# Fewer loads at the head of a retention and soft-mixture kernel: eight of them issued later, by ScalarE

## The chip, the cores and the metric

The kernel runs on one core of one Trainium2 chip. Its time is the device time of one execution in microseconds (us); the median of the runs is what counts. A core has five engines that run their own instruction streams and meet through semaphores: TensorE (PE, matrix products; PEld is its loading of stationary operands), VectorE (DVE), ScalarE (ACT), GpSimd (POOL) and SyncE (SP, which here only issues DMAs). Data come from HBM into SBUF through 16 DMA engines; products arrive in PSUM, which has eight banks.

## The reference

Two stages follow each other for batch 8, 8 heads, 576 positions and head width 64. The first is retention, causal attention without a softmax, with a decay by distance for each head:

```python
scores = scale * np.matmul(q, k.transpose(0, 1, 3, 2))
gamma = 1.0 - 2.0 ** (-5.0 - np.arange(H, dtype=np.float32))
Dmat = np.where(rel >= 0, gamma[:, None, None] ** rel[None, :, :], 0.0)
x = np.matmul(scores * Dmat[None], v)      # then (B, S, 512)
```

The second takes x (8 x 576 x 512) through four attention experts of width 64, of which each position uses the best two by a gate:

```python
logits = x @ w_gate                        # best 2 of 4, weights by softmax
for e in range(E):
    q = x @ wq[e]; k = x @ wk[e]; v = x @ wv[e]
    a = softmax(causal(scale * (q @ k.transpose(0, 2, 1))))
    out += gate_weight[e] * (a @ v @ wo[e])
```

All is float32. The inputs are q, k, v of the first stage (laid out as tiles `xf` and `vkf` before the launch) and the weights (`wraw`).

## The kernel before

The positions are cut into 36 tiles of 128 (`NT`), three of which form a group (`NG` = 12 groups). The program is one loop over j (groups, with three more rounds to drain) and i (0 to 2), so that tile n = 3j + i passes through the first stage while the projections of group j − 1, the scores of group j − 2 and the output of group j − 3 are worked on.

For tile n in the first stage these functions are called, in this order around the loop: `qk(n+1)` (products of q and k of the tile on TensorE, copied out of PSUM by ScalarE into `p`, line 144, and masked by GpSimd, line 147), `old(n)` (the part from the running state, copied out by ScalarE, line 169), `own(n)` (the part from the tile itself, added by VectorE, lines 187 and 188), `state(n+1)` (the running state; TensorE, then adds on VectorE, line 128), `scale(n)` (decay factors from the table `gi`, line 200; VectorE for the first three tiles, GpSimd after), `split(n)` (rounding into a high part `xh` by ScalarE, line 210, and its remainder `xl` by GpSimd, line 211), `table(n+1)` (the next piece of the table, four small activations, line 99) for the first tiles, and `decay` (line 107), which multiplies the v of a later tile by powers of the decay, on VectorE for tiles 0 to 2, on GpSimd behind. For n = 2 `qk(3)` stands behind `own(2)` instead of ahead of `old(2)`.

`weights(w)` (line 227) rounds one of the four weight matrices into a high and a low part in the same way: ScalarE makes the high part (`wh`, line 235), VectorE or, for `q`, GpSimd the low one (`wl`, line 236). `k` is done after tile 1, `q` and `v` after tile 2, `o` after tile 5. With `v` goes the gate's small matrix `rg`. `proj` (`pj`, line 250) needs `k` and `q` and all three tiles of its group and first runs in the round n = 3; `vproj` (`pv`, line 274) needs `v` and first runs at n = 4.

Loads: `load(n, 0)` brings the q and k of a tile (`x`, 512 KB, three buffers), `load(n, 1)` its v and k in another layout (`vk`, 512 KB, four buffers), `fetch(w)` a weight matrix (`raw`, 512 KB). All are issued on SyncE. A load into a buffer that is in use waits for its last reader: `x3` takes the buffer of `x0`, which `old(0)` reads last, `x4` that of `x1`, and `vk4` that of `vk0`.

What sets the order: the instructions of TensorE, VectorE, ScalarE and GpSimd run in the order in which the program writes them (`ORDERED`). SyncE's order is chosen by the planner of the framework, which may put a load that is ready ahead of one that still waits. PSUM is handed out as eight banks in turn (`bank`), so that a new product waits for whoever empties the bank that was taken eight calls before.

Of the kernel before, what the change touches and what calls it, by code (L numbers as in the profile page):

```python
# [27 lines left out]
def f(ap):  # L28
    return ap.bitcast(F32)
# [9 lines left out]
def units(g):  # L39
    out = []  # L40
    for n in range(3 * g, 3 * g + 3):
        out += [(n, 0), (n, 1)] if n % 9 == 8 else [(n, None)]
    return out
# [3 lines left out]
def kernel(ctx: ExitStack, tc: tile.TileContext, xf, vkf, wraw, gi_d, con_d, out):  # L47
    nc = tc.nc
# [8 lines left out]
    v = nc.vector  # L57
# [25 lines left out]
    HALF = [slice(0, 64), slice(64, 128)]  # L83
    X, VK, P, S_, XR = {}, {}, {}, {}, {}

    def load(n, w):
        if n >= NT:
            return
        if w == 0:
            X[n] = x = ld.tile([128, 2, 4, 128], F32, name="x", tag="x")  # L90
            nc.sync.dma_start(x, xf[n])
        else:
            VK[n] = vk = ld.tile([128, 2, 2, 4, D], F32, name="vk", tag="vk", bufs=4)
            nc.sync.dma_start(vk, vkf[n])

    def table(c):
        t0, C = 128 * c, 128 if c < 4 else 64
# [3 lines left out]
    def decay(n, e=None):  # L101
        if n >= NT:
            return
        vv = VK[n][:, :, 0]
        k = chunks(n)[0][1]
        gm = gam[:, 8:9] if k == 8 else gam[:, k:k + 2]
        (e or gp).tensor_mul(vv, vv, gm.unsqueeze(3).to_broadcast([128, 2, 4, D]))  # L107
# [22 lines left out]
    def qk(n):  # L130
        if n >= NT:
            return
        x = X[n]
        ps = [bank([128, 2, 2, 64], "qk") for g in range(2)]
        for s in range(2):
            i = slice(64 * s, 64 * s + 64)
            for u in range(2):
                for g in range(2):
                    for r in range(2):
                        h = 2 * r + u  # L140
                        mm(ps[g][HALF[r], s, u], x[HALF[g], 1, h, i], x[HALF[g], 0, h, i], start=True, stop=True)  # L141
        P[n] = p = sa.tile([128, 2, 2, 2, 64], F32, name="p", tag="p")
        for g in range(2):
            act(p[:, g], ps[g], AF.Copy)  # L144
        for r in range(2):
            w = p[HALF[r]].rearrange("p g s u i -> p (g s u) i")
            gp.affine_select(w, w, pattern=[[0, 8], [1, 64]], base=0, channel_multiplier=-1,  # L147
                             compare_op=OP.is_ge, fill=0.0)
# [3 lines left out]
    def old(n):  # L152
        if n >= NT:
            return
        ps = [bank([128, 2, 128], "old") for g in range(2)]
        x = X[n]
        R[n] = x32 = sa.tile([128, 2, 2, 128], F32, name="x32", tag="x32", bufs=2)
        ch = chunks(n)
        f0 = 64 if ch[0][1] == 0 else 0
        for s, (b, k) in enumerate(ch):  # L160
            i = slice(64 * s, 64 * s + 64)
            if k:
                for r in range(2):
                    for g in range(2):
                        for u in range(2):
                            mm(ps[g][HALF[u], r, i], S_[b, k - 1][HALF[g], r, u], x[HALF[g], 0, 2 * r + u, i],  # L166
                               start=True, stop=True)
        for g in range(2):
            act(x32[:, g, :, f0:], ps[g][:, :, f0:], AF.Copy)

    def own(n):
        if n >= NT:
            return
        ps = [bank([128, 2, 128], "own") for r in range(2)]
        p, vk, x32 = P.pop(n), VK[n], R[n]
        ch = chunks(n)
        f0 = 64 if ch[0][1] == 0 else 0
        for s in range(2):
            i = slice(64 * s, 64 * s + 64)
            for g in range(2):  # L180
                for r in range(2):
                    for u in range(2):
                        mm(ps[r][HALF[u], g, i], vk[HALF[r], s, 0, 2 * g + u], p[HALF[r], g, s, u],  # L183
                           start=True, stop=True)
        for r in range(2):
            if f0:
                v.tensor_copy(x32[:, :, r, :f0], ps[r][:, :, :f0])
            v.tensor_add(x32[:, :, r, f0:], x32[:, :, r, f0:], ps[r][:, :, f0:])  # L188

    def scale(n, e=None):  # L190
        if n >= NT:
            return
        e = e or gp
        x32 = R[n].rearrange("p g r i -> p (g r) i")
        k = chunks(n)[0][1]
        if k == 8:
            w = x32.rearrange("p c (s i) -> p c s i", s=2)
            e.tensor_mul(w, w, gi[:, :, 512:].unsqueeze(2).to_broadcast([128, 4, 2, 64]))
        else:
            e.tensor_mul(x32, x32, gi[:, :, 64 * k:64 * k + 128])  # L200

    def split(n, e=None):
        if n >= NT:
            return
        g, l0 = n // 3, 128 * (n % 3)
        if n % 3 == 0:
            XR[g] = (sa.tile([128, 4, GW], F32R, name="xh", tag="xh"), sa.tile([128, 4, GW], F32R, name="xl", tag="xl"))
        xh, xl = XR[g]
        x32 = R.pop(n).rearrange("p g r i -> p (g r) i")
        act(xh[:, :, l0:l0 + 128], x32, AF.Copy)  # L210
        (e or gp).tensor_sub(xl[:, :, l0:l0 + 128], x32, f(xh[:, :, l0:l0 + 128]))  # L211
# [6 lines left out]
    TSZ = {1: 11 * 128, 2: 15 * 128, 3: 9 * 128, 4: 9 * 128}  # L218
    rg = const.tile([128, 4, E], F32, name="rg")

    def fetch(w):
        o, kc, n = WCUT[w]
        z = {"k": 1, "q": 2, "v": 3, "o": 4}[w]
        RAW[w] = raw = sb.tile([128, PSZ[z]], F32, name="raw", tag=f"p32{z}")[:, :kc * n].rearrange("p (k w) -> p k w", k=kc)
        nc.sync.dma_start(raw, wraw[:, o:o + kc * n].rearrange("p (k w) -> p k w", k=kc))

    def weights(w, e=None):
        o, kc, n = WCUT[w]
        raw = RAW[w]
        wt = n if w != "v" else NWV  # L230
        hi = const.tile([128, kc, wt], F32R, name="wh" + w)
        lo = const.tile([128, kc, wt], F32R, name="wl" + w)
        W[w] = (hi, lo)
        for r, cs in [(raw, slice(0, n))] + ([(rg, slice(n, wt))] if w == "v" else []):
            act(hi[:, :, cs], r, AF.Copy)
            (e or v).tensor_sub(lo[:, :, cs], r, f(hi[:, :, cs]))
# [248 lines left out]
    def stage(j, i):  # L485
        g, o = j - 1, j - 3
        if 0 <= g < NG:
            if i == (0 if j == 1 else 2):
                for p in range(2):
                    for w in "kq":  # L490
                        yield from proj(g, w, p)
            else:
                for ti in (2,) if i == 1 else (0, 1):
                    yield from vproj(3 * g + ti)
        if 0 <= o < NG and i < 2:
            for d in (2 * i, 2 * i + 1):
                yield from outproj(o, d)
# [8 lines left out]
    load(2, 0)  # L506
    load(2, 1)
    fetch("k")
    fetch("q")
    nc.sync.dma_start(rg, wraw[:, 4096:].rearrange("p (k w) -> p k w", k=4))  # L510
    load(3, 1)
    fetch("v")
    nc.sync.dma_start(mask[:, 512:], con_d[:, 220:])
    decay(0, v)
    qk(0)
# [1 line left out]
    for j in range(NG + 3):  # L517
        us = units(j - 2) if 0 <= j - 2 < NG else []
        for i in range(3):
            n = 3 * j + i  # L520
            if n < 2:
                decay(n + 1, v)
            if n != 2:
                qk(n + 1)
            old(n)
            work = stage(j, i)
            here = us[i:i + 1] if i < 2 else us[2:]
            soft = [scores(u) for u in here[:1]]
            for sc in soft:
                next(sc)  # L530
            own(n)
            if n == 2:
                qk(3)
            state(n + 1)
            for u in here[1:]:
                soft.append(scores(u))
                next(soft[-1])
            load(n + 3, 0)
            load(n + 4, 1)
            if n == 0:  # L540
                fetch("o")
            scale(n, v if n < 3 else None)
            if 2 < n + 2 and i < 2:
                decay(n + 2)
            for u, sc in zip(here, soft):
                for _ in sc:
                    next(work, None)
                normal(u)
            split(n)
            if 0 < n + 1 < 5:  # L550
                table(n + 1)
            if i == 2:
                decay(n + 2)
            if n == 1:
                weights("k")
            if n == 2:
                weights("q", gp)
                weights("v")
            if n == 5:
                weights("o")  # L560
            run(work)
        for u in us:
            run(turn(u))
        if 0 <= j - 1 < NG:
            gate(j - 1)
        for u in us:
            values(u, u[0] == NT - 1)
# [56 lines left out]
```

## Time and profile before

| | |
|---|---|
| median of three runs | 470.75 us (470.01 to 472.14) |
| the profiled execution | 470.5 us |
| its span, first to last instruction | 468.5 us |
| mean granted TensorE clock | 0.967 |
| HBM read, written | 40.26 MB, 9.44 MB |

The profile is that of one execution. Its page gives each engine's busy time and groups of instructions by line; the timeline lists instructions in order of time, neighbours of one line merged, each with its start, its length, the engine, what it writes and reads, and in square brackets the idle time ahead of it with what ended it. "issue" there means that the engine waited for nothing that the profile shows. Issuing a DMA is not counted as busy time of an engine. Of the DMAs the page says how long they took from issue to landing. The clock column gives the share of full TensorE speed that was granted. The profiled execution took 2.0 us more than its span, for what lies around the first and last instruction.

### The profile page before, as it was taken

Reading aid. Unit: us, or ns where it says so; the run is one execution under the profiler, and the core shown is the slowest. Engines: PE = TensorE matmul, PEld = TensorE weight load, DVE = VectorE, ACT = ScalarE, POOL = GpSimd, SP = SyncE. Lnnn points to the kernel's source line nnn. Section 1 sums busy time; section 2 is a strip of 40 time slices with the busy share of each in tenths; the row PEclk is TensorE's granted clock in tenths of the full one; section 3 lists DMA queues with packets and bytes.
Section 4 is the critical chain, followed back from the end, with each engine's and each line's share of the span. In section 5 each row is a group of like instructions: output and inputs, shape, how many; then the busy total and the mean of one; then the engine's idle time right before and its main releaser. Section 6 shows DMA issues by size and latency. Waiting matters only on the chain.

```text
span 468.5 us, 18762 instructions
## 1 busy us (share of the span) xinstructions
PE 436.8 (93%) x7876; PEld 397.9 (85%) x7876; DVE 273.0 (58%) x1069; ACT 286.4 (61%) x834; POOL 216.1 (46%) x272
## 2 busy tenths in 40 slices
PE   7589879999999999999999999999999999999786
PEld 4478769889879989889979999889979999897476
DVE  1562773864685654864775654854775654746650
ACT  2545466584685476584686576685686576664752
POOL 5477665563653555563653455553553453202001
PEclk8769899999999999999999999999999999999869
DMA  8953441242252153252352153242241010010101
GB/s 286 406 200 105 171 135 48 93 160 91 92 186 65 50 186 110 92 165 86 94 167 83 41 193 111 92 163 88 93 162 44 5 52 18 2 69 2 69 0 69
DMA packets 18899, 50.89 MB, mean 109 GB/s; under 512 B 2304, under 2 KB 9088, under 8 KB 18816
## 3 DMA queue, kind: packets, MB, share of 16 engines
q1 hardware_dynamic: 18816, 49.71, 31.3%
q8 instruction: 62, 1.02, 0.9%
q14 instruction: 21, 0.17, 0.1%
HBM read 40.26 MB, written 9.44 MB: 106 GB/s over the span
## 4 chain that ended last, share of the span: by engine, by line
PE 79%; ACT 7%; DVE 4%; DMA 4%; issue 3%; POOL 1%; SPq 1%; ACTq 0%; POOLq 0%; DVEq 0%
PE pj L250 22%; PE pv L274 11%; PE pt L419 8%; PE po L473 8%; PE ss L348 7%; PE ys L445 6%; PE own L183 4%; DMA x<-xf 4%; PE qk L141 4%; PE st L119 3%; PE old L166 2%; ACT p L379 2%; PE ys L452 2%; DVE sm L391 2%; PE ys L449 2%
## 5 line engine op out<-in xcount | busy, mean ns | idle before, releaser
L211 POOL TENSOR_TENSOR xl<-x,xh 128x512 fp32r<-128x512 f32 x36 | 46.1, 1280 | 89.3 <-ACT xh L210 89.3
L379 ACT ACTIVATE p<-p,nm 128x128 f32<-128x128 f32 (+8 forms) x144 | 79.7, 559 | 10.4 <-DVE nm L368 9.5
L368 DVE CUSTOM_DVE_ANT_0 p<-ss,mask 128x128 f32<-128x128 f32 (+7 forms) x128 | 51.0, 454 | 29.0 <-PE ss L348 28.5
L463 POOL CAST yh<-y 128x256 fp32r<-128x256 f32 (+1 forms) x38 | 14.4, 380 | 106.4 <-ACT y L462 106.4
L399 ACT ACTIVATE p<-p,sm 128x64 f32<-128x64 f32 (+4 forms) x72 | 37.0, 556 | 42.0 <-DVE sm L393 42.0
L423 DVE COPY pth<-pt 128x512 f32<-128x512 f32 (+2 forms) x52 | 31.4, 618 | 48.2 <-PE pt L419 47.8
L147 POOL TENSOR_SCALAR_AFFINE_SELECT p<-p 64x512 f32<-64x512 f32 x72 | 48.7, 676 | 20.3 <-ACT p L144 17.7
L419 PE MATMUL pt<-con,p 128*128 128x128 f32 x360 | 45.1, 287 | 5.4 <-DVE nm L373 3.3
L419 PEld LDWEIGHTS pt<-con,p 128*128 128x128 f32 x360 | 43.3, 149 | 6.1 <-DVE nm L373 3.4
L200 POOL TENSOR_TENSOR x<-x,gi 128x512 f32<-128x512 f32 x29 | 37.4, 1290 | 20.4 <-DVE x L188 19.5
L348 PE MATMUL ss<-k,q 64*64 64x64 f32 (+7 forms) x512 | 41.7, 409 | 2.2 <-ACT ot L476 2.2
L183 PEld LDWEIGHTS own<-p,vk 64*64 64x64 f32 x1152 | 28.5, 142 | 13.4 <-issue 10.4
L445 PE MATMUL ys<-pth,vn 128*64 128x128 f32 (+1 forms) x640 | 39.8, 257 | 0.0
L183 PE MATMUL own<-p,vk 64*64 64x64 f32 x1152 | 30.4, 229 | 6.6 <-ACT xh L210 2.8
L107 POOL TENSOR_TENSOR vk<-vk,con 128x512 f32<-128x512 f32 x33 | 35.4, 1074 | 0.3 <-DMA vk<-vkf 0.3
L391 DVE TENSOR_SCALAR sm<-sm 128x4 f32<-128x4 f32 (+1 forms) x40 | 15.5, 388 | 30.6 <-ACT p L379 30.0
L425 ACT ACTIVATE pth<-pt 128x512 f32<-128x512 f32 (+2 forms) x52 | 27.2, 541 | 9.3 <-PE pt L419 9.3
L210 ACT ACTIVATE xh<-x 128x512 fp32r<-128x512 f32 x36 | 22.2, 617 | 17.2 <-POOL x L200 9.6
L445 PEld LDWEIGHTS ys<-pth,vn 128*64 128x64 f32 x640 | 29.6, 139 | 1.5 <-issue 1.5
L401 DVE TENSOR_SCALAR p<-p,sm 128x64 f32<-128x64 f32 (+4 forms) x104 | 29.1, 333 | 1.4
L141 PEld LDWEIGHTS qk<-x 64*64 64x64 f32 x1152 | 21.6, 141 | 9.6 <-issue 7.0
L119 PE MATMUL st<-vk 64*64 64x64 f32 x1024 | 25.8, 232 | 4.3 <-DVE vk L107 2.2
(94 smaller groups left out, 1069.8 us busy)
## 6 DMA issues: line engine op xcount, KB each, us to landing
x<-xf SPq DMA_DIRECT2D x36, 512.0 KB, 4.0
vk<-vkf SPq DMA_DIRECT2D x36, 512.0 KB, 5.3
out<-ot SPq DMA_DIRECT2D x48, 192.0 KB, 2.0
raw<-wraw SPq DMA_DIRECT2D x4, 512.0 KB, 9.4
gi<-gi SPq DMA_DIRECT2D x1, 256.0 KB, 8.1
con<-con SPq DMA_DIRECT2D x1, 110.0 KB, 3.9
mask<-con SPq DMA_DIRECT2D x1, 32.0 KB, 8.5
rg<-wraw SPq DMA_DIRECT2D x1, 8.0 KB, 9.3
```

The source lines that it names most:

```text
L119: mm(ps[r][HALF[g], s, u], vk[HALF[r], s, 1, h], vk[HALF[r], s, 0, h], start=True, stop=True)
L141: mm(ps[g][HALF[r], s, u], x[HALF[g], 1, h, i], x[HALF[g], 0, h, i], start=True, stop=True)
L147: gp.affine_select(w, w, pattern=[[0, 8], [1, 64]], base=0, channel_multiplier=-1, compare_op=OP.is_ge, fill=0.0)
L183: mm(ps[r][HALF[u], g, i], vk[HALF[r], s, 0, 2 * g + u], p[HALF[r], g, s, u], start=True, stop=True)
L211: (e or gp).tensor_sub(xl[:, :, l0:l0 + 128], x32, f(xh[:, :, l0:l0 + 128]))
L250: mm(ps, ww[:, kc, p * 128:(p + 1) * 128], xx[:, kc, c], start=(i == 0), stop=(i == 11))
L274: mm(ps, xx[:, kc, l0:l0 + 128], ww[:, kc], start=(i == 0), stop=(i == 11))
L348: mm(ps[e][HALF[p]], q[p][HALF[z], l0 + 64 * s:l0 + 64 * s + 64], k[p][HALF[z], kb:kb + ws[e]], start=True, stop=True)
L368: v.tensor_tensor_reduce(p32[:, e, :ws[e]], ps[e], mask[:, 576 - ws[e]:], -1.0, BIG, OP.add, OP.min, nm[:, e:e + 1])
L379: act(p32[:, e, :ws[e]], p32[:, e, :ws[e]], AF.Exp, bias=bias[e], scale=-1.0, accum_out=sm[:, 0, e:e + 1])
L419: nc.tensor.transpose(pt[:, i], src, ident)
L445: mm(py[HALF[z], p], VN[n0 + j][:, e * D:(e + 1) * D], src, start=(j == 0), stop=False)
```

## The change

Ahead of the loop, the loads of `rg` and `v` are gone and `load(3, 0)` is called there. In the loop, `load(n+3, 0)` and `load(n+4, 1)` are called on SyncE only from n = 3 on. The loads of `x4`, `vk4`, `rg` and `v` are issued by ScalarE behind `split(1)`, and those of `x5`, `vk5`, `vk6` and `o` behind `split(2)`, in each case ahead of `table`. `weights("v")` moves from n = 2 to n = 3, behind `table(4)`.

```diff
-    def load(n, w):
+    def load(n, w, e=None):
+        e = e or nc.sync
...
-            nc.sync.dma_start(x, xf[n])
+            e.dma_start(x, xf[n])
...
-            nc.sync.dma_start(vk, vkf[n])
+            e.dma_start(vk, vkf[n])
...
-    def fetch(w):
+    def fetch(w, e=None):
...
-        nc.sync.dma_start(raw, wraw[:, o:o + kc * n].rearrange("p (k w) -> p k w", k=kc))
+        (e or nc.sync).dma_start(raw, wraw[:, o:o + kc * n].rearrange("p (k w) -> p k w", k=kc))
...
     fetch("k")
     fetch("q")
-    nc.sync.dma_start(rg, wraw[:, 4096:].rearrange("p (k w) -> p k w", k=4))
+    load(3, 0)
     load(3, 1)
-    fetch("v")
     nc.sync.dma_start(mask[:, 512:], con_d[:, 220:])
...
-            load(n + 3, 0)
-            load(n + 4, 1)
-            if n == 0:
-                fetch("o")
+            if n > 2:
+                load(n + 3, 0)
+                load(n + 4, 1)
             scale(n, v if n < 3 else None)
...
             split(n)
+            if n == 1:
+                load(4, 0, nc.scalar)
+                load(4, 1, nc.scalar)
+                nc.scalar.dma_start(rg, wraw[:, 4096:].rearrange("p (k w) -> p k w", k=4))
+                fetch("v", nc.scalar)
+            if n == 2:
+                load(5, 0, nc.scalar)
+                load(5, 1, nc.scalar)
+                load(6, 1, nc.scalar)
+                fetch("o", nc.scalar)
             if 0 < n + 1 < 5:
                 table(n + 1)
...
             if n == 2:
                 weights("q", gp)
+            if n == 3:
                 weights("v")
```

## The prediction, made before the changed kernel was run

> **What bounds the kernel now.** I read the page first, then busy time by stage.
>
> ```profile
> span 468.5 us, 18762 instructions
> ```
>
> ```profile
> 0.00:32.00 32.00, 21.24 (x574) 17.04 (x575) 12.77 (x33) 14.62 (x38) 17.38 (x35) 0.74 0.83 305
> 200.00:400.00 200.00, 196.69 (x3667) 182.43 (x3668) 121.54 (x492) 131.38 (x386) 97.76 (x116) 1.00 0.29 97
> ```
>
> The two rows are stretches of the run; behind the length stand busy time of PE, PEld, DVE, ACT, POOL, then granted clock, DMA share and GB/s. From 200 to 400 us TensorE is busy for 196.69 of 200 us, so nothing but TensorE counts there. In the first 32 us it is busy for 21.24, at a mean clock of 0.74, and the DMA engines are at 0.83. This head is all that the change touches; I take it that what follows the first projection shifts with the projection's start. So the question is: when does the first projection (`pj`) start, and at which clock? The timeline of the head, engine by engine, answers the first half: TensorE, ScalarE, VectorE, GpSimd (start, length, then what ran, and in brackets the wait before it).
>
> ```profile
> 21.61 1.05 PE L183 MATMUL own<-p,vk 64*64 64x64 f32 x32 [2.77 <-ACT xh L210]
> ...
> 25.79 1.12 PE L141 MATMUL qk<-x 64*64 64x64 f32 x28 [0.57 <-DMA x<-xf]
> 28.42 0.37 PE L141 MATMUL qk<-x 64*64 64x64 f32 x2 [1.51 <-issue]
> ...
> 30.32 1.14 PE L119 MATMUL st<-vk 64*64 64x64 f32 x30
> 31.39 1.35 PE L250 MATMUL pj<-xh,whk 128*128 128x384 f32 x4
> ```
>
> ```profile
> 20.01 0.63 ACT L210 ACTIVATE xh<-x 128x512 fp32r<-128x512 f32 x1 [2.91 <-DVE x L200]
> 20.55 1.26 ACT L99 ACTIVATE gi<-gi,con 128x128 f32<-128x128 f32 x4
> 21.71 1.04 ACT L235 ACTIVATE whk<-raw 128x1024 fp32r<-128x1024 f32 x1
> 22.66 0.63 ACT L169 ACTIVATE x<-old 128x256 f32<-128x256 f32 x2
> 24.38 0.66 ACT L144 ACTIVATE p<-qk 128x256 f32<-128x256 f32 x2 [1.09 <-PE qk L141]
> 27.11 0.63 ACT L210 ACTIVATE xh<-x 128x512 fp32r<-128x512 f32 x1 [2.07 <-DVE x L200]
> 27.65 1.26 ACT L99 ACTIVATE gi<-gi,con 128x128 f32<-128x128 f32 x4
> 28.82 1.04 ACT L235 ACTIVATE whq<-raw 128x1024 fp32r<-128x1024 f32 x1
> 29.76 1.04 ACT L235 ACTIVATE whv<-raw 128x1024 fp32r<-128x1024 f32 x1
> 30.71 0.20 ACT L235 ACTIVATE whv<-rg 128x16 fp32r<-128x16 f32 x1
> 30.81 0.63 ACT L144 ACTIVATE p<-qk 128x256 f32<-128x256 f32 x2
> ```
>
> ```profile
> 22.79 1.22 DVE L236 TENSOR_TENSOR wlk<-raw,whk 128x1024 fp32r<-128x1024 f32 x1 [2.87 <-ACT whk L235]
> 23.93 0.74 DVE L188 TENSOR_TENSOR x<-x,own 128x256 f32<-128x256 f32 x2
> 25.23 0.88 DVE L128 TENSOR_TENSOR s<-st,s 128x128 f32<-128x128 f32 x4 [0.56 <-PE st L119]
> 26.04 0.98 DVE L200 TENSOR_TENSOR x<-x,gi 128x512 f32<-128x512 f32 x1
> ```
>
> ```profile
> 27.89 1.27 POOL L211 TENSOR_TENSOR xl<-x,xh 128x512 fp32r<-128x512 f32 x1 [1.41 <-ACT xh L210]
> 29.11 1.04 POOL L107 TENSOR_TENSOR vk<-vk,con 128x512 f32<-128x512 f32 x1
> ```
>
> Three routes arrive at the first projection (31.39) almost together. **TensorE's own:** its waits of 2.77, 0.57 and 1.51 us in front of `own(2)`, `qk(4)` and the last of `qk(4)`; then it works on without a pause past 31.39. **GpSimd's:** the rounding of tile 2 (`xh`, 27.11), its remainder `xl` (27.89), the decay of `vk4` (29.11, done at 30.15), and at once `state(4)` on TensorE. **ScalarE's:** from 20.01 to 23.29 without a gap (`xh`, table, `whk`, eviction of `old(2)`); `whk` lets VectorE make `wlk` (22.79), behind which stand the adds of `own(2)` and `state(3)` and the scaling (26.04); that gives `xh` of tile 2 at 27.11, and again ScalarE without a gap up to `p(4)` at 30.81. Counted from the code, the eight PSUM banks go round, and the first projection takes the one that `p(4)` empties. So a shorter wait on TensorE alone brings the projection forward by nothing: GpSimd's and ScalarE's routes must get shorter too. The change works on the first and puts eight DMA issues into the other two.
>
> **The change, part by part.**
>
> *Lighter queue.* Up to the load of `q` the order is the old one.
>
> ```profile
> GB/s 0 270 307 302 364 388 411 403 390 409 420 393 412 412 391 73 23 91 281 229 12 0 0 0 208 377 197 293 152 0 197 187 213 12 0 16 272 183 173 253
> ```
>
> ```profile
> x<-xf SPq DMA_DIRECT2D x36, 512.0 KB, 4.0
> ```
>
> The first row gives the rate in 40 slices of the first 70 us, 1.75 us each: about 400 GB/s to 26.25 us. The new head loads ten tiles and weights of 512 KB and small tables, some 5.6 MB; the first ten slices sum to 3,244 GB/s, times 1.75 us is 5.7 MB. So traffic ends at about 17.5 us instead of 26.25. `load(3,0)` is no early load in fact: its buffer is that of `x0`, which `old(0)` must have read, so it queues behind that on SyncE, as before. The waits for x and the 2.77 and 1.51 us, which fall into the saturated stretch (the second is marked "issue", the first names a ScalarE row that was over 0.97 us earlier), can shrink: between 0 and all of their 4.85 us. I expect `own(2)` about 2 us earlier, and `x4`, issued by ScalarE at 20.1 and landing 4.0 us later by the last row, at 24.1 instead of 25.8. Worth at the projection: 0, since the other routes don't use it. If this cover is absent (both others earlier), it is worth up to 4.85.
>
> *What VectorE gains.* The add of `state(3)` waited 0.56 us for TensorE. With `state(3)` earlier this wait goes: −0.56 on both other routes.
>
> *First block of four issues* (`x4`, `vk4`, `rg`, `v`), behind `xh` of tile 1 and ahead of the table for tile 2. No row shows a DMA issued by ScalarE. The nearest are SyncE's:
>
> ```profile
> 2.67 0.43 SPq L94 DMA_DIRECT2D vk<-vkf  x1
> 3.14 0.65 SPq L505 DMA_DIRECT2D gi<-gi  x1
> ...
> 16.87 0.33 SPq L91 DMA_DIRECT2D x<-xf  x1
> 17.30 0.37 SPq L94 DMA_DIRECT2D vk<-vkf  x1
> ```
>
> Each takes 0.33 to 0.43, starts lie 0.43 to 0.47 apart, and 0.65 is seen where six had been issued in a row. Four at 0.47 are 1.9 us. ScalarE starts its next activation 0.54 us after `xh` (20.01 to 20.55); if issuing, which the profile doesn't count as engine work, runs in that time too, the block holds up the next activation by c = 1.9 − 0.54 = 1.35. Bounds: four at 0.33 less 0.54 is 0.78; four at 0.65 without overlap 2.6; nothing at all is the lower end if issue runs wholly beside. I take 1.35, as the queues are nearly empty there, as in the first rows. Their buffers (`x1`, `vk0`) were read long before, so ScalarE should not block on them. Behind the block on ScalarE stand table 2, `whk`, the eviction of `old(2)`; VectorE waits for `whk`. So `xh` of tile 2 moves by 1.35 − 0.56 = +0.79, to 27.90; `xl`, the decay and `state(4)` move with it, and `state(4)` starts at 31.0. TensorE, ahead now, waits there some 3 us.
>
> The Trainium skill, DMA: Bandwidth & Descriptors, section "Issuing engines are not separate DMA queues", says that issuing from several engines saves only the sequencer's time to initiate, which is usually small beside the transfer. By it both blocks would count as small, c near 0; no run here shows a ScalarE issue yet, and SyncE's rows say 1.9 us for four.
>
> *Second block* (`x5`, `vk5`, `vk6`, `o`), behind `xh` of tile 2: another 1.35, ahead of table 3, `whq` and `p(4)`. The weights `v` leave this place: −(30.81 − 29.76) = −1.05, `p(4)` starting in the place of `whv`. Its first half of 0.33 ends at 29.76 + (c − 0.56) + c + 0.33 = 29.53 + 2c, which is 32.23. GpSimd's route gives 31.39 + 0.79 = 32.18. Projection at 32.2: **+0.8**. The readers of this block's transfers (`qk(5)`, the decays of `vk5` and `vk6`, the rounding of `o`) come behind the start of the projection, which covers at least the 4.0 us to landing: 0, or a microsecond or two if the landing takes as long as in the full queue. SyncE's own queue, left with `x6` and `vk7` there, loses nothing.
>
> *Weights `v` one tile later.* `whv` and its tail (1.04 + 0.20) now stand behind table 4, on VectorE behind `own(3)`.
>
> ```profile
> 30.84 2.73 DVE L236 TENSOR_TENSOR wlv<-raw,whv 128x1024 fp32r<-128x1024 f32 x1 [3.82 <-ACT whv L235]
> ```
>
> ```profile
> 36.80 1.05 ACT L99 ACTIVATE gi<-gi,con 128x64 f32<-128x64 f32 x4
> ```
>
> ```profile
> 42.81 0.64 PE L274 MATMUL pv<-wlv,xh 128*128 128x260 f32 x4
> ```
>
> ```profile
> 30.00:32.00 2.00, 2.00 (x53) 1.88 (x46) 1.16 (x1) 1.98 (x6) 2.00 (x2) 0.50 0.62 178
> 32.00:34.00 2.00, 2.00 (x13) 2.00 (x12) 2.00 (x2) 0.00 (x0) 2.00 (x2) 0.94 0.88 248
> ```
>
> Table 4 ends at 37.85; with some 0.8 us of shift and 1.24 of work `whv` is ready at 39.9, and `wlv` 2.7 us later at 42.6 (1.22 if it goes as fast as `wlk`). Its reader moves from 42.81 to at least 43.6. Nothing is lost, by a cover of 1 us; without it, 1 to 2 us.
>
> *Clock.* The last two rows show 0.50 before 32 us and 0.94 over the next two, so full clock from 32 + 2·0.12 = 32.24, 3.8 us after TensorE set out at 28.42 without further pause. After the change it arrives early at `state(4)`, stands still and sets out at 31.0; by the same 3.8 us it is slow until 34.8. Slow projection time grows from 0.85 us (31.39 to 32.24) to 2.6 (32.2 to 34.8); at half clock half of the difference is lost: **+0.9**. Bounds: 0 and 2.0 (slow to 37 us).
>
> The Trainium skill, TensorE: Matmul & The Clock Gate, Part 1, has a free-running window of about 3.4 us, full clock following a busy one. Its estimate is full clock between 34.4 and 37.8 us, so +0.7 to +2.4 for this term and 472.0 to 473.7 in all; the trace's 3.8 us fits, and the phase is not known.
>
> *Sum:* the profiled execution took 470.5 us (468.5 of span and 2.0 around it), 0.25 below the median of three, 470.75 (470.01 to 472.14). 470.5 + 0.8 + 0.9 = **472.2**, 0.3% above the median. About 0.5% (2.35 us) is what a measurement of this kernel can tell from no change.
>
> **Rivals.**
>
> *Slower: issues hold ScalarE in full.* With no overlap c is 1.9, and with 0.65 each 2.6. Then ScalarE's route decides: 29.53 + 2c is 33.33 or 34.73, so +1.9 or +3.3, and with the clock's 0.9 the time is 473.3 to 474.7. The projection moves by 29.53 + 2c − 31.39 = 2c − 1.86, so it counts as slower from c = 1.78 on (2c − 1.86 + 0.9 = 2.6, which is 2.35 above the median). For it: an engine that issues does nothing else in its program order. Against: the profile counts issuing apart from engine work, so the activation ahead of it may run on beside it. Chance 0.38.
>
> *Issues cost nothing.* c = 0: both routes come 0.56 earlier, the projection at 30.83; 470.5 − 0.56 + 0.9 = 470.8, without the clock's loss 469.9. For it: the profile shows no ScalarE issue that costs anything; against: SyncE's rows. Chance 0.10. The rule of the Trainium skill on issuing engines, above, would make it this case.
>
> *Faster: the early wait goes too.* An "issue" wait stands at the end of `old(1)`'s first matmuls:
>
> ```profile
> 15.09 0.98 PE L166 MATMUL old<-x,s 64*64 64x64 f32 x28 [1.76 <-issue]
> ```
>
> `scale(1)` and so `xh` of tile 1 hang on it; without it all routes move by 1.76. With cheap issues: 469.9 − 1.76 = 468.1, faster. Against: the queues are as full at 13 us in both kernels. Chance 0.10.
>
> *The loads of the head don't matter at all*, since `x3` waits for its buffer as before and TensorE's own route isn't the only one: this is inside my forecast.
>
> **How the numbers follow.** Forecast 0.42: by its bounds (c from 0.78 to 1.6, clock 0 to 1.3) 470.7 to 473.1. Same = 0.42 + 0.10 = 0.52; slower 0.38; faster 0.10. The range leaves out the faster case (0.10) and the top of the slower one: 469.4 (469.9 less half a microsecond of spread) to 475.0.
>
> **What would show it.** Right: traffic falls off near 17.5 us; `own(2)` starts before 20; the table's activations stand 1.8 to 2 us behind `xh` at tiles 1 and 2; `state(4)` waits for the decay after a pause of TensorE; projection near 32.2, clock 0.50 to about 35; no wait at `pv<-wlv`. Wrong: the table 0.6 us behind `xh` (issues free), or over 2.4 (the slower case); the 1.76 us gone; a projection before 31; or a DMA wait on ScalarE.

## The result and the profile after

| | before | after |
|---|---|---|
| median of the runs (12 each) | 470.61 us (469.21 to 472.79) | 473.82 us (471.63 to 496.33) |
| ratio | 1 | 1.0051, 95% interval 1.0030 to 1.0073 |
| profiled execution, span | 470.5, 468.5 | 471.63, 469.9 |

The changed kernel is slower by 0.5%, about 2.4 us by the ratio (1.4 to 3.4 by its interval); the two medians lie 3.2 us apart. (The run of 496.33 was disturbed and is left out of the ratio.) The forecast was 472.2, with 469.4 to 475.0 as its range. The median of 473.82 is above the forecast's own bounds (up to 473.1) and inside the slower rival's (473.3 to 474.7); by the ratio, 470.75 × 1.0051 = 473.15, it stands on the line between the two. Line numbers after are one higher than before. Where the time went shows in the head. First TensorE, in the timeline after:

```profile
19.33 0.75 PE L184 MATMUL own<-p,vk 64*64 64x64 f32 x30 [0.38 <-POOL vk L108]
...
25.32 0.95 PE L142 MATMUL qk<-x 64*64 64x64 f32 x32 [4.11 <-ACT x L170]
26.64 1.34 PE L167 MATMUL old<-x,s 64*64 64x64 f32 x30 [0.38 <-DVE x L189]
...
31.49 1.23 PE L120 MATMUL st<-vk 64*64 64x64 f32 x32 [2.55 <-POOL vk L108]
33.15 1.65 PE L251 MATMUL pj<-xh,whk 128*128 128x384 f32 x4 [0.42 <-ACT p L145]
34.59 1.48 PE L251 MATMUL pj<-xh,wlk 128*128 128x384 f32 x4
35.87 1.11 PE L251 MATMUL pj<-xl,whk 128*128 128x384 f32 x4
36.81 0.87 PE L251 MATMUL pj<-xh,whq 128*128 128x384 f32 x4
...
43.24 0.70 PE L142 MATMUL qk<-x 64*64 64x64 f32 x32
```

TensorE is ahead at `own(2)` (19.33 instead of 21.61) and gets nothing for it: it waits 4.11 us for ScalarE, 2.55 for the decay on GpSimd and 0.42 for `p(4)`. The first projection starts at 33.15 instead of 31.39, and its first three groups of four take 1.65, 1.48 and 1.11 us, where they take 0.97, 0.86 and 0.86 at full speed ("TensorE kept busy" below). So `qk(5)`, the first work behind it, comes at 43.24; before, it came 2.86 us sooner:

```profile
40.38 0.69 PE L141 MATMUL qk<-x 64*64 64x64 f32 x32
```

Then ScalarE after; ACTq is the issuing of DMAs on it:

```profile
19.87 0.63 ACT L211 ACTIVATE xh<-x 128x512 fp32r<-128x512 f32 x1 [2.67 <-DVE x L201]
19.90 0.38 ACTq L92 DMA_DIRECT2D x<-xf  x1
20.37 0.38 ACTq L95 DMA_DIRECT2D vk<-vkf  x1
20.80 1.45 ACTq L552 DMA_DIRECT2D rg<-wraw  x1
22.28 0.44 ACTq L226 DMA_DIRECT2D raw<-wraw  x1
22.77 1.28 ACT L100 ACTIVATE gi<-gi,con 128x128 f32<-128x128 f32 x4 [2.27 <-issue]
23.95 1.04 ACT L236 ACTIVATE whk<-raw 128x1024 fp32r<-128x1024 f32 x1
24.90 0.63 ACT L170 ACTIVATE x<-old 128x256 f32<-128x256 f32 x2
25.43 0.65 ACT L145 ACTIVATE p<-qk 128x256 f32<-128x256 f32 x2
28.40 0.63 ACT L211 ACTIVATE xh<-x 128x512 fp32r<-128x512 f32 x1 [2.33 <-DVE x L201]
28.43 0.33 ACTq L92 DMA_DIRECT2D x<-xf  x1
28.86 0.88 ACTq L95 DMA_DIRECT2D vk<-vkf  x2
29.77 0.78 ACTq L226 DMA_DIRECT2D raw<-wraw  x1
30.60 1.28 ACT L100 ACTIVATE gi<-gi,con 128x128 f32<-128x128 f32 x4 [1.57 <-issue]
31.79 1.04 ACT L236 ACTIVATE whq<-raw 128x1024 fp32r<-128x1024 f32 x1
32.73 0.63 ACT L145 ACTIVATE p<-qk 128x256 f32<-128x256 f32 x2
```

The first issue begins 0.03 us after `xh` has begun, so the two do overlap. But the next activation begins only when the last issue of its block has ended (22.72 and 30.55): 2.90 us behind the start of `xh` at tile 1 and 2.20 at tile 2, where before it was 0.54 at both. That is 2.36 and 1.66 us more. Then the DMA rate in 40 slices of the first 70 us, GpSimd, and two stretches of 2 us, in which the first of the last three numbers is the granted clock and the second the share of the DMA engines:

```profile
GB/s 0 284 223 311 393 392 405 410 402 357 73 28 302 398 185 9 68 360 379 412 414 178 0 0 0 35 318 267 309 295 2 30 265 206 108 0 73 236 47 250
```

```profile
29.18 1.26 POOL L212 TENSOR_TENSOR xl<-x,xh 128x512 fp32r<-128x512 f32 x1 [1.66 <-ACT xh L211]
30.39 1.04 POOL L108 TENSOR_TENSOR vk<-vk,con 128x512 f32<-128x512 f32 x1
```

```profile
34.00:36.00 2.00, 2.00 (x8) 2.00 (x7) 1.54 (x6) 0.00 (x0) 1.94 (x3) 0.50 1.01 406
36.00:38.00 2.00, 2.00 (x12) 2.00 (x11) 0.00 (x0) 0.00 (x0) 1.92 (x3) 0.90 0.79 311
```

Traffic drops in the eleventh slice, at 17.5 us, as worked out. GpSimd runs in the old order, `xl` 29.18 instead of 27.89. The clock is at 0.50 up to 36 and at 0.90 over the next two, so full from 36 + 2·0.2 = 36.4 us, 4.9 us after TensorE set out at 31.49.

The lag grows a little more on the way. At the last first-group of a projection it is 2.91 us:

```profile
413.74 0.97 PE L250 MATMUL pj<-xh,whk 128*128 128x384 f32 x4
```

```profile
416.65 0.97 PE L251 MATMUL pj<-xh,whk 128*128 128x384 f32 x4
```

Yet the two spans differ by 1.4 only. The rest lies in the tail, where in the stretch 452 to 456 the execution before (first row) had a spell of slow clock that the one after (second row) did not have there:

```profile
452.00:456.00 4.00, 4.00 (x44) 3.67 (x44) 1.93 (x4) 1.81 (x5) 0.00 (x0) 0.57 0.00 0
```

```profile
452.00:456.00 4.00, 1.81 (x16) 1.65 (x18) 3.61 (x10) 3.31 (x9) 0.00 (x0) 1.00 0.00 0
```

Such spells (0.43 of 4 us is 1.7 us of work) fall differently in each execution. The execution profiled after was the fastest of its twelve. Hence, below, the start of `qk(5)` is read from the profiles for what the head does, and the time from the ratios of all the runs.

### The profile page after: what moved, and what is told of

It is laid out like the page before. It is cut to its first block, busy times and chain, and to the rows that moved or that the text cites. A ratio compares the mean times of both kernels' runs of the same rounds, so it can differ in the third digit from the quotient of the medians.

```text
span 469.9 us, 18762 instructions
## 1 busy us (share of the span) xinstructions
PE 434.9 (93%) x7876; PEld 395.2 (84%) x7876; DVE 269.6 (57%) x1069; ACT 286.3 (61%) x834; POOL 215.0 (46%) x272
## 4 chain that ended last, share of the span: by engine, by line
PE 76%; ACT 9%; DVE 6%; issue 3%; DMA 2%; POOL 1%; SPq 1%; ACTq 1%; DVEq 0%; POOLq 0%
PE pj L251 22%; PE pv L275 10%; PE pt L420 8%; PE po L474 7%; PE ss L349 6%; PE ys L446 6%; PE own L184 4%; PE qk L142 3%; PE st L120 3%; ACT p L380 2%; PE old L167 2%; PE ys L453 2%; DMA raw<-wraw 2%; PE ys L450 2%; DVE sm L392 1%
## 5 line engine op out<-in xcount | busy, mean ns | idle before, releaser
L148 POOL TENSOR_SCALAR_AFFINE_SELECT p<-p 64x512 f32<-64x512 f32 x72 | 47.6, 660 | 22.7 <-ACT p L145 20.1
L420 PE MATMUL pt<-con,p 128*128 128x128 f32 x360 | 43.4, 280 | 6.2 <-DVE nm L374 3.3
L420 PEld LDWEIGHTS pt<-con,p 128*128 128x128 f32 x360 | 41.6, 145 | 7.2 <-DVE nm L374 3.4
L349 PE MATMUL ss<-k,q 64*64 64x512 f32 (+7 forms) x512 | 42.0, 410 | 2.3 <-ACT ot L477 2.3
L392 DVE TENSOR_SCALAR sm<-sm 128x4 f32<-128x4 f32 (+1 forms) x40 | 14.2, 355 | 30.6 <-ACT p L380 30.0
L189 DVE TENSOR_TENSOR x<-x,own 128x256 f32<-128x256 f32 (+1 forms) x72 | 25.4, 386 | 9.4 <-ACT x L170 8.1
```

What stands on the lines that cost most here:

```text
L349: mm(ps[e][HALF[p]], q[p][HALF[z], l0 + 64 * s:l0 + 64 * s + 64], k[p][HALF[z], kb:kb + ws[e]], start=True, stop=True)
L420: nc.tensor.transpose(pt[:, i], src, ident)
```

## The experiments

Theory: the issues hold ScalarE, and what hangs on ScalarE is late; the pause that TensorE makes for it keeps its clock low. Rivals: the loads themselves come too late; the weights `v` one tile later cost; the lighter head costs. Each ratio is to the kernel before, run on the same chip in the same job; the median of before was 471.57 to 472.03 there, and 470.61 beside the changed kernel, so compare kernels by ratios and not by medians. The starts are those of the one profiled execution of each.

| kernel | median us | ratio (95%) | projection starts | `qk(5)` starts |
|---|---|---|---|---|
| before | | 1 | 31.39 | 40.38 |
| after | 473.82 | 1.0051 (1.0030 to 1.0073) | 33.15 | 43.24 |
| issues alone | 476.12 | 1.0079 (1.0051 to 1.0108) | 35.03 | 46.46 |
| both blocks ahead | 471.95 | 0.9989 (0.9961 to 1.0016) | 30.31 | 41.16 |
| loads on SyncE | 472.41 | 1.0004 (0.9976 to 1.0033) | 31.30 | 41.88 |
| TensorE kept busy | 472.84 | 1.0011 (0.9989 to 1.0034) | 33.02 | 41.63 |
| `rg` at the head | 472.28 | 1.0017 (0.9986 to 1.0048) | 31.96 | 42.10 |
| `rg` first, one execution | 472.91 | | 33.07 | 43.62 |
| `v` later, alone | 472.83 | 1.0014 (0.9985 to 1.0043) | 31.05 | 41.01 |
| spread | 471.46 | 0.9986 (0.9960 to 1.0012) | 29.81 | 39.86 |
| spread, kept busy | 471.31 | 0.9984 (0.9956 to 1.0013) | 31.14 | 39.75 |
| spread, decay early, six products | 470.51 | 0.9972 (0.9948 to 0.9996) | 29.94 | 38.59 |
| before, `v` later, decay early | 469.48 | 0.9944 (0.9918 to 0.9971) | 31.10 | 40.78 |
| before, decay early | 471.88 | 1.0007 (0.9979 to 1.0034) | 31.41 | 40.06 |

**The issues alone.** To the kernel before, eight small DMAs that nobody reads:

```diff
...
+    def idle(i):
+        nc.scalar.dma_start(scr[i], wraw[:, 4096:4100])
...
             split(n)
+            if n == 1:
+                idle(0)
+                idle(1)
+                nc.scalar.dma_start(scr4, wraw[:, 4096:].rearrange("p (k w) -> p k w", k=4))
+                idle(2)
+            if n == 2:
+                for z in range(3, 7):
+                    idle(z)
```

> The kernel before with its own loads untouched, and eight more DMAs issued by ScalarE at the places of the change: they bring 2 or 8 KB each into tiles that nobody reads. Theory (ScalarE's issue time is the price): the activation behind the first block starts about 2.3 us later and the one behind the second about 1.5 us; p(4) moves from 30.8 to about 34, the first projection from 31.4 to about 34.4, the clock loses about 1 us more, and the time rises by 3 to 4 us (ratio 1.006 to 1.009). Rival (the loads come too late, the issue costs nothing): the loads are those of before, so the time is that of before, 470.6, ratio 1.000 within 0.002.

The tables on its ScalarE, behind the two blocks, and its projection:

```profile
22.39 1.28 ACT L99 ACTIVATE gi<-gi,con 128x128 f32<-128x128 f32 x4 [1.79 <-DMA x<-xf]
...
31.43 1.28 ACT L99 ACTIVATE gi<-gi,con 128x128 f32<-128x128 f32 x4 [2.79 <-DMA scr<-wraw]
```

```profile
35.03 1.65 PE L255 MATMUL pj<-xh,whk 128*128 128x384 f32 x4 [2.68 <-ACT p L144]
```

0.8% slower, with the loads where they were: issuing on ScalarE is enough to lose what the change lost and more, and late loads are not needed for it. How much of it is issuing proper this kernel does not say: behind its second block the table stands 3.42 us behind `xh` (28.01 to 31.43) instead of 2.20, since the issues also waited for earlier DMAs to land, as the bracket says; and `whv` still stands ahead of `p(4)`. The projection waited 2.68 us for `p(4)` alone.

**Both blocks ahead of the rounding.** The changed kernel with the two `if` blocks above `split(n)` instead of below it:

```diff
-            split(n)
             if n == 1:
                 load(4, 0, nc.scalar)
...
                 fetch("o", nc.scalar)
+            split(n)
```

> The kernel after with both blocks of issues ahead of the rounding of tiles 1 and 2 instead of behind it: there ScalarE stood idle for 2.67 and 2.33 us in the kernel after. Theory (issue time on ScalarE's route): most of both blocks is hidden in that idle time, the first projection goes back from 33.15 to about 30.8 to 31.5 and the time to 469.5 to 471 (ratio 0.998 to 1.001). Rival (what costs is that weights v were moved, or the lighter head): nothing of that is changed, so the time stays near 473.8 (ratio 1.006).

The eight issues are the same; the time is that of before, and the projection starts 2.84 us earlier than after the change. So neither the later weights nor the lighter head is what costs. Only the first block ran mostly in ScalarE's idle time. The second, which the program has behind the table, `whk` and the evictions of `old(2)` and `qk(3)`, was issued beside them, without a gap between them:

```profile
20.61 0.34 ACTq L92 DMA_DIRECT2D x<-xf  x1
20.72 0.68 ACT L100 ACTIVATE gi<-gi,con 128x128 f32<-128x128 f32 x2
...
21.60 1.04 ACT L236 ACTIVATE whk<-raw 128x1024 fp32r<-128x1024 f32 x1
21.95 0.69 ACTq L226 DMA_DIRECT2D raw<-wraw  x1
```

So here an issue held up the activations behind it in the program (after the change), and not those ahead of it that had not run yet. `qk(4)` has a new wait in its middle:

```profile
25.87 0.37 PE L142 MATMUL qk<-x 64*64 64x64 f32 x2 [2.06 <-issue]
```

The earlier loads brought it; "spread" below follows it up.

**The same loads on SyncE.** `nc.scalar` replaced by `nc.sync` in the two blocks.

> The kernel after with the eight loads issued by SyncE, in the same place of the program. Theory: ScalarE's route is free of issues and of the weights v, GpSimd's route decides, projection at about 30.8; TensorE waits there, so some clock may be lost; time 469.5 to 471 (ratio 0.998 to 1.001). Rival (lighter head or later weights v cost): near 473.8.

The time is that of before; ScalarE's route is as it was before or shorter (`p(4)` at 29.68 instead of 30.81). Issued by SyncE the loads start as soon as their buffers are free, so the queue is full again until 26 us, and TensorE's waits are back (2.83 us ahead of `own(2)`). The projection starts at 31.30, not at the 30.8 expected.

**TensorE kept busy in its pause.**

```diff
     def state(n):
...
         ps = [bank([128, 2, 2, D], "st") for r in range(2)]
+        if n == 4:
+            for i in range(11):
+                mm(ps[0], wz, wz[:, None, :].to_broadcast([128, 2, 128]).rearrange("p a (b c) -> p a b c", b=2), start=True, stop=True)
```

> The kernel after with eleven products of zeros on TensorE ahead of state(4), into the bank that state(4) overwrites, to fill its pause of 2.55 us. Theory (the pause keeps the clock at half, which costs about 1.1 us of the projection): the first projection starts near 33.1 as in the kernel after, but at full clock, so that it ends about 1 us sooner; time 472.3 to 473 (ratio 1.004 to 1.005). Rival (the clock's phase is set otherwise, or the loss is made up later): slow clock in the projection as before it, or the same time as after, 473.8 (ratio 1.006 to 1.007).

```profile
28.99 2.43 PE L117 MATMUL st<-wz 128*128 128x256 bf16 x11
31.62 0.79 PE L123 MATMUL st<-vk 64*64 64x64 f32 x32 [0.20 <-POOL vk L108]
33.02 0.97 PE L254 MATMUL pj<-xh,whk 128*128 128x384 f32 x4 [0.61 <-ACT p L148]
33.83 0.86 PE L254 MATMUL pj<-xh,wlk 128*128 128x384 f32 x4
```

The projection starts at almost the same time, 0.13 us earlier, but at full speed (0.86 instead of 1.48 for the second group), and `qk(5)` comes at 41.63 instead of 43.24. So 1.5 us of the 2.9 lost at `qk(5)` come back when the pause is filled: that is the clock's part. The ratio falls from 1.0051 to 1.0011, below the 1.004 to 1.005 expected; the two were measured in different jobs, and their intervals just overlap.

**`rg` at the head; `rg` first.** Two runs on the 1.45 us of one issue. In the first, `rg` goes back to SyncE ahead of the loop, in the second (one execution) it stands first in the block.

> The kernel after with the small load of rg (512 pieces of 16 bytes) back at the head on SyncE, so that ScalarE's first block has three issues. In the kernel after the issue of rg took 1.45 us, where x4 and vk4 took 0.38 each. Theory A (rg's many small pieces are what made it long): the block gets 1.5 us shorter, the first projection comes at about 31.9 to 32.1 instead of 33.15, and the time is 471.5 to 472.5 where the kernel after would give 473.8 (ratio 1.002 to 1.004 to before). Theory B (the third issue in a row is long whatever it is, because the two ahead of it are still being worked off): the load of v takes the 1.45 in its place, the block gets only 0.5 us shorter, projection at about 32.7, ratio 1.004 to 1.006.

> The kernel after with rg first in ScalarE's first block, x4, vk4 and v behind it. If rg itself takes the 1.45 us, its issue is long in the first place too, and x4 goes out 1 us later; if it is the place behind two full loads, rg takes 0.3 to 0.5 and one of the others 0.8 to 1.5. The block as a whole takes 2.3 to 2.9 us in either case and the first projection comes at 32.7 to 33.3.

The first blocks of the two, in this order:

```profile
19.76 0.38 ACTq L92 DMA_DIRECT2D x<-xf  x1
20.23 0.39 ACTq L95 DMA_DIRECT2D vk<-vkf  x1
20.66 0.44 ACTq L226 DMA_DIRECT2D raw<-wraw  x1
```

```profile
19.77 0.38 ACTq L550 DMA_DIRECT2D rg<-wraw  x1
20.25 0.38 ACTq L92 DMA_DIRECT2D x<-xf  x1
20.73 0.39 ACTq L95 DMA_DIRECT2D vk<-vkf  x1
21.16 1.56 ACTq L226 DMA_DIRECT2D raw<-wraw  x1
```

`rg` itself takes 0.38, so its many small pieces are not what is long, and theory A is wrong as it was put. But three issues without `rg` run through in 1.34 us, and theory B is wrong too: the load of `v` takes 0.44 right behind two full loads. Four take 2.9, one of them 1.5. With three the projection came at 31.96, near the 32.2 of the forecast, and the ratio at 1.0017. What the long one waits for stays open. The first blocks of the two hold 1.34 and 2.95 us, but in the first kernel `vk5` and `vk6` took 1.62 us in the second block, and the table stood 2.64 us behind `xh` there instead of 2.20.

**The weights `v` later, alone.** To the kernel before, `weights("v")` under `if n == 3`.

> The kernel before with one part of the change alone: the rounding of the weights v one tile later. Theory (a gain on ScalarE's route alone, p(4) 1.05 us earlier, but GpSimd's route and TensorE's own stay): first projection at 31.3 to 31.5 as before, no new wait at the first product with wlv, ratio 0.998 to 1.002. Rival (this part costs, since whv and wlv now stand between the table and the evictions of the projection): projection as before but a wait of 1 us or more at the first vproj, ratio 1.003 or more.

The ratio's interval includes 1; the projection starts 0.34 us earlier, and the first product with `wlv` did not wait. This part of the change costs nothing that these runs can tell from noise, as forecast.

**Spread.** Fewer of the early loads, ahead of the rounding. The two blocks of the changed kernel become:

```python
            if n == 1:
                load(4, 0, nc.scalar)
                load(4, 1, nc.scalar)
            if n == 2:
                load(5, 0, nc.scalar)
                load(5, 1, nc.scalar)
                nc.scalar.dma_start(rg, wraw[:, 4096:].rearrange("p (k w) -> p k w", k=4))
                fetch("v", nc.scalar)
            split(n)
```

with `vk6` and `o` on SyncE in the round n = 3.

> The kernel after with the issues in ScalarE's idle time ahead of the rounding, and fewer of them: x4 and vk4 ahead of the rounding of tile 1, x5, vk5, rg and v ahead of that of tile 2, vk6 and o on SyncE in the round of tile 3. With all eight ahead (the kernel with both blocks ahead of the rounding) the projection came 1.08 us earlier than before, but the last products of qk(4) waited 2.06 us for nothing the profile shows, in the traffic of those loads. Theory (that wait is the fetching of TensorE's instructions through the same DMA engines): the wait shrinks to under 0.7 us, with traffic near nothing from about 20 to 23 us; state(4) still waits for the decay on GpSimd until about 29.1, so the projection stays at about 30.3 and the time at a ratio of 0.996 to 1.001. Rival (the wait has another cause, ScalarE or GpSimd): 1.5 to 2.1 us of wait in the same place.

The wait in `qk(4)` is gone, as expected, but one of 1.96 us is back ahead of `own(2)`, now that `x4` and `vk4` are issued at 16.00 and 16.48:

```profile
20.78 1.14 PE L184 MATMUL own<-p,vk 64*64 64x64 f32 x30 [1.96 <-ACT xh L211]
```

The DMA view has a queue of its own for instructions. Cut into half microseconds it shows when a packet of it moved (packets, MB, share of the engines' time); the spread kernel from 18.0 to 18.5 us:

```profile
q8 instruction: 1, 0.02, 13.6%
```

There TensorE goes on at 20.78. The same line stands at 19.0 to 19.5 before (TensorE goes on at 21.61), at 23.5 to 24.0 with both blocks ahead (25.87), and at 16.5 to 17.0 after the change (`own(2)` at 19.33). In each case TensorE goes on 2.4 to 2.8 us behind the start of the packet's half microsecond, wherever the packet moves to; with the second packet before (25.5 to 26.0, TensorE at 28.42) it is 2.9. And the places are fixed: counted in the traces, together with the semaphore and branch instructions that do no work on the engine, the waits at 15.09, 21.61 and 28.42 before stand at TensorE's 450th, 706th and 962nd instruction, 256 apart. The 15.37 after the change, the 20.78 here and the 25.87 with both blocks ahead stand at the same three. That speaks for waits for instructions, and against the ScalarE row in the bracket of `own(2)`, which is named in some kernels only; no run took the fetching away by itself. The Trainium skill, Runtime: NRT & Kernel Launch, section "Instruction fetch mechanics", says that each engine's instructions come in blocks of 256 through a DMA queue of its own and that the cost is mostly hidden. The blocks agree (the 256 above; 15,752 rows of PE and PEld on 62 packets, 254 each, without those instructions); that the cost is hidden does not hold in this head, by these waits, where a block of small products lasts only about 4 us (before, from 15.09 to the end of `old(2)` at 18.85) and the next comes through a full queue.

**Spread, kept busy.** The same with fourteen products of zeros ahead of `state(4)`.

> The kernel of the spread issues with fourteen products of zeros on TensorE ahead of state(4), in its pause. Theory (the clock is what is left of the loss once the issues are hidden): projection at about 30 to 30.6, at full clock within a microsecond, so that the tile behind it starts 1 us or more earlier than in the kernel before; time 1 to 2.5 us below before, ratio 0.995 to 0.998. Rival (the clock gets slow again later and gives it back): ratio 0.999 to 1.001.

Full speed in the projection from its start, as expected, but `qk(5)` at 39.75 is 0.63 us ahead of before and not the 1 us or more expected: the projection starts at 31.14, as all of the head ran 1.4 us later in this execution (`xh` of tile 1 at 21.17). The ratio misses the 0.995 to 0.998 expected, and its interval includes 1: undecided.

**Decay early.** `decay(4)` needs only its load, so it can go earlier. Three kernels move the decay of `vk4` ahead of the rounding of tile 2 in GpSimd's order: the spread one (with six products of zeros), the one before with `v` later, and the one before alone.

```diff
+            if n == 2:
+                decay(4)
             split(n)
...
-            if i == 2:
+            if i == 2 and n > 2:
                 decay(n + 2)
```

> The kernel of the spread issues, with the decay of vk4 ahead of the rounding of tile 2 in GpSimd's order (it needs only its load) and six products of zeros ahead of state(4). Theory (with the issues hidden and TensorE early, GpSimd's route is the last, then ScalarE's p(4)): state(4) no longer waits for the decay, the first projection starts when p(4) is out, at about 29 instead of 29.8, at or near full clock; the tile behind it (qk(5)) starts at 38 to 39 where the kernel before has 40.38; time 1 to 2.5 us below before, ratio 0.995 to 0.998. Rival (a start of the projection earlier by one or two us is lost in the run's later spells of slow clock): ratio 0.998 to 1.001 with the same early qk(5).

> The kernel before with the weights v rounded one tile later and the decay of vk4 ahead of the rounding of tile 2: both other routes shorter, the loads as before. Theory (three routes arrive together before; with the full queue TensorE's own, with its waits of 2.8 and 1.5 us, stays): the first projection starts where own(3) and state(4) allow it, at 30.8 to 31.5, ratio 0.998 to 1.001. Rival (TensorE's waits are no bound, ScalarE and GpSimd alone are): projection at 30 or earlier, ratio 0.996 or less.

> The kernel before with one edit: the decay of vk4 ahead of the rounding of tile 2. The kernel that also rounds the weights v later came out at a ratio of 0.9944, though its profiled execution started the projection only 0.29 us earlier. Theory A (the early decay alone does it, since GpSimd's route falls away): ratio 0.993 to 0.997. Theory B (both routes must be short: p(4) stays in the place behind whv): projection at 31.1 to 31.5, ratio 0.998 to 1.002. If it is B's ratio, it stays open how much of the 0.9944 is chance of the clock's spells.

First products of the projection, in the same order:

```profile
29.94 0.97 PE L254 MATMUL pj<-xh,whk 128*128 128x384 f32 x4 [0.21 <-ACT p L148]
```

```profile
31.10 1.65 PE L250 MATMUL pj<-xh,whk 128*128 128x384 f32 x4
```

```profile
31.41 0.97 PE L250 MATMUL pj<-xh,whk 128*128 128x384 f32 x4 [0.62 <-ACT p L144]
```

With the early decay alone the projection waits for `p(4)`: one route shortened, the next one decides, no gain. With both shortened and the old loads, TensorE's own route decides and the projection waits for nobody (31.10). With the loads spread as well, it starts at 29.94 at full speed. By their intervals the first, only just, and the second are faster than the kernel before. But their order is not the one expected: the second was to be 0.998 to 1.001 and has 0.9944, with `qk(5)` at 40.78 in its profiled execution, which with 471.89 us was the second slowest of its twelve. Its profile does not show where 2.6 us come from in the others; that stays open.

## Why the prediction was right, and by how much it was off

**Three routes, and a lighter queue that buys nothing: right.** `own(2)` came before 20 us (19.33), traffic ended at 17.5, `state(4)` waited for the decay. Priced at 0, and so it was: TensorE waited 4.11 + 2.55 + 0.42 us for the others. One detail was off: `qk(4)` waited not for `x4` but for the eviction of `old(2)` by ScalarE. The faster rival did not come: the wait at 15.09 before stood at 15.37 after, with 1.81 us.

**VectorE's 0.56 us: right,** and 0.30 more: the scaling took 0.68 instead of 0.98.

**The issues: the mechanism right, the term mis-sized.** Forecast: c, the time by which a block holds up the next activation, is 1.35, as four issues at 0.47 less 0.54 of overlap. Measured: 2.36 and 1.66. The overlap was there (0.03 us between the starts), against the rival's ground; what was off is the assumption that all four issues take what the first ones on SyncE took. A row of 0.65 had been weighed, but the issue right behind it on SyncE, in the kernel before, takes 1.45:

```profile
3.83 1.45 SPq L91 DMA_DIRECT2D x<-xf  x1
```

On ScalarE `rg` took 1.45, and in the second block `vk5` and `vk6` took 0.88 together and `o` 0.78. So the bound of 0.65 for each was no bound for a single issue; the rival's 2.6 for a block held. By the forecast's own formula 29.53 + 2.36 + 1.66 is 33.55; `p(4)` began at 32.73, which with the same 0.33 puts the end of its first half at 33.06, 0.5 earlier, mainly by the quicker scaling (0.30) and `xh` of tile 1 (0.14). The projection moved by 1.76, where 0.8 was forecast and 1.9 was the slower rival's lower price. That rival decided from a mean c of 1.78 on; the mean was 2.01. The forecast's own sign of it, the table over 2.4 us behind `xh`, showed at tile 1 (2.90) and not at tile 2 (2.20). The rule of free issues, that issuing from another engine saves only a time that is small beside the transfer (the Trainium skill, DMA: Bandwidth & Descriptors, "Issuing engines are not separate DMA queues"), agrees for the single issue: most took 0.33 to 0.44 us here, and their transfers landed 4.4 to 7.1 us after the issue (medians). What the prediction drew from it for both blocks, c near 0, does not hold: on the bounding route the issues of a block add up.

**`v` later: right,** no wait at `wlv`; alone within the noise.

**The clock: right, by a rule that did not hold.** Forecast +0.9 with full speed from 34.8; it came at 36.4, and between the start of the projection and `qk(5)` 1.1 us more were lost (2.86 − 1.76). From setting out to full speed it took 4.9 us, not the 3.8 of before; the prediction's wider estimate, 34.4 to 37.8, holds the 36.4. The price came out nearly right all the same, because the projection started later too: it was slow for 3.25 us (33.15 to 36.4) instead of the 2.6 forecast. Kept busy, the same projection ran at full speed from its start.

**The sum:** 1.76 + 1.1 = 2.9 instead of 0.8 + 0.9 = 1.7 at `qk(5)`; the ratio says 2.4 (1.4 to 3.4). Direction and mechanism were forecast, the size was nearer to the slower rival's: "slower by over 0.5%" had 0.38, and 1.0051 lies a hair past that line, with an interval that leaves both sides open. That the range holds 473.82 is owed to its having taken in most of that rival.

## What to carry to other kernels

Before a DMA is given to an engine because it "has time", look whether that engine's next instruction is on the bounding route: here an issue held what stood behind it for 0.3 to 1.6 us, and the same eight issues cost nothing that could be measured when they stood ahead of the instruction for whose input the engine waits. Where several routes arrive together, shortening one only makes another the last, and a pause that this gives TensorE can cost about as much again in clock (here 1.5 of the 2.9 us lost at `qk(5)`). Loads put off to lighten a queue come back as traffic later; TensorE's waits, which look like waits for its instructions, came back with such traffic in three kernels here (2.06, 2.83 and 1.96 us).

## What the runs showed of the hardware that had not been expected

A block of four issues of the real loads took 1.9 to 3.0 us on ScalarE in every kernel that had one, the longest issue in it 0.5 to 1.6 us and at changing places, while three ran through in 1.34. Issues ran beside activations that stood ahead of them in the program and had not run yet (20.61 to 22.64 with both blocks ahead). And in a head of small products, under a full queue, TensorE stood for up to some 3 us at a time in waits that stand 256 instructions apart and move with its instruction packets.
